# Loads of V issued by SyncE's queue in place of ScalarE's, in an attention and expert kernel

## The chip, the cores and the metric

The kernel runs on one core of a Trainium2 chip. The metric is the device time of one execution in microseconds, the median over several runs. The core's engines each work through their own instructions in a fixed order and wait for each other by semaphores: TensorE (PE in the profile; PEld are its weight loads), VectorE (DVE), ScalarE (ACT), GpSimd (POOL) and SyncE (SP), which does nothing but issue transfers. ACT and POOL can issue transfers too. All transfers of the core are carried by its 16 DMA engines.

## What is computed

Attention over 4 batches of 8 heads with 768 positions and 64 dimensions, in which a query sees only the keys with the same 6-bit hash; then, per batch, the 128 positions with the highest gate score go through one two-layer expert and are added back.

```python
q_bits = (np.einsum('bhsd,dk->bhsk', q, proj) > 0)      # same for k_bits
mask = q_bucket[:, :, :, None] == k_bucket[:, :, None, :]
scores = np.where(mask, scale * np.matmul(q, k.transpose(0, 1, 3, 2)), -1000000000.0)
scores = scores - np.max(scores, axis=-1, keepdims=True)
attn = np.exp(scores)
attn = attn / (np.sum(attn, axis=-1, keepdims=True) + 1e-09)
out = np.matmul(attn, v)                                 # heads side by side: x
top_idx = np.argpartition(-scores[b], capacity)[:capacity]   # scores[b] = x[b] @ w_gate
h = np.maximum(xe @ w1, 0.0)                             # xe = x[b, top_idx]
out[b, top_idx] = x[b, top_idx] + g[:, None] * (h @ w2)
```

## The kernel before

The 32 heads are worked through one after the other, each over all 768 positions, with several heads in flight. A head h has these steps:

- SP loads its queries and keys into X (`load_x`, line 379, 384 KB). ACT rounds them to half precision (XH, line 501), DVE takes the rest (XL, line 506). PE hashes X (line 473), DVE makes signs of it (sg, sd, lines 490 to 497).
- SP moves the pieces into the operands of the matmuls, within the core's memory, all through `move` (line 513): the signs into A and K (`A<-sg`, `K<-sd`), the halves into A (`A<-XH`), the difference of key halves into K (`K<-xd`), and both into B (`B<-A`, `B<-XL`). There are four buffers each of A and K and two of B.
- PE computes an upper bound for each row's score (`max_unit`, line 649), ACT and DVE take its maximum (me, line 657; mj, line 666), PE turns it (line 676), ACT casts it into `mr` (line 681), and SP moves this row of maxima into row 96 of A (`max_row`, the transfer `A<-mr`, 1.5 KB).
- PE computes the scores `st` with A (line 697) and B (line 701), with the maximum taken off in the same matmul; the line 697 matmuls can't start before `A<-mr` has landed. ACT takes the exp into P (lines 715 and 717), DVE or POOL its rounding rest R (lines 732 and 735), and PE multiplies P and R by V into `av` (line 760). ACT scales the result into x (line 784).

V is loaded for two heads at a time (`load_v`, line 382, 16 loads of 384 KB). The tile that a load lands in has one buffer (`bufs=1`), so a load has to wait until DVE has read the pair before from it. ACT splits the load into the upper halves (`split_vh`, line 562), DVE into the lower ones (`split_vl`, line 568), into one of two operand tiles.

In between run the steps of the expert: its weights W are loaded in 8 pieces of 512 KB by ACT's queue (lines 808 and 813), finished halves of x are written out by ACT's queue (line 829), and the scores make a round trip through memory on SP's queue (lines 870 and 873).

What sets the order is a table, `ORDER`, that lists all steps; the steps are issued in this order to all engines, and each engine, and each queue of transfers, keeps it. A transfer is issued by the engine that the line names, at its place among that engine's own instructions. An engine that comes to a transfer whose inputs or buffer aren't ready stands still there, and so does all that is behind it.

Of the kernel before, what the change touches and what calls it, by code (L numbers as in the profile page):

```python
# [41 lines left out]

WARM = (34, 24, 6, 6)
POOL_R = ((1,), (0, 2), ())
ACT_V = True
ACT_W = True
TURNS = True
PJW = 66
# [196 lines left out]
def body(ctx, tc, qk, v, pj, wg, w1, w2, cst, out):  # L245
# [136 lines left out]
    def load_v(pr):  # L382
        t = sb.tile([P, NC, 2, D], F32, tag="V", name=f"V{pr}", bufs=1)
        (nc.scalar if ACT_V else nc.sync).dma_start(t, v[pr])
        st["V", pr] = t
# [918 lines left out]
```

## Time and profile before

| | before |
|---|---|
| median of 3 runs | 417.01 us (414.02 to 419.23) |
| profiled execution | 415.9 us, span 414.1 us |
| PE busy | 392.2 us, 95% |
| DVE busy | 352.4 us, 85% |
| ACT busy | 332.8 us, 80% |
| POOL busy | 181.6 us, 44% |
| SP's queue of transfers (q1) | 35.58 MB, 31.4% of the 16 DMA engines' span |
| ACT's queue of transfers (q10) | 16.45 MB, 12.6% |
| mean granted TensorE clock | 0.996 |

The span runs from the first to the last instruction; the profiled execution's time is 1.8 us longer. PE is close to busy throughout, but matmuls overlap and their ends are modelled, so the places where another engine's wait ends tell more than the share. Of SP the profile shows no busy time, only when it issued what. Where a time of the trace stands with two decimals it is counted from the start of the span.

### The profile page before, as it was taken

The page shows a single profiled execution, that of the slowest core. Times are in us where ns is not written, and L with a number is a line of the kernel's source. Part 1 is how long each engine was busy: PE and PEld are TensorE (multiplying, and loading weights), DVE is VectorE, ACT ScalarE, POOL GpSimd, SP SyncE. Part 2 cuts the span into 40 slices and gives each one's busy share as a digit, 9 for nine tenths or more (in the row PEclk, how much of TensorE's full clock was granted, in tenths as well). Part 3 has the DMA queues.
Part 4 walks back from the last instruction along what each step waited for, and adds up shares of the span by engine and source line. Part 5 has one row for each costly group of instructions (what it writes and reads, how often), then busy time and mean ns, then how long its engine had stood idle before and what let it go on. Part 6 is the DMA issues. An engine that isn't in the chain of part 4 may idle for free. (4 is left out here: it accounts for less than half of the span.)

```text
span 414.1 us, 14588 instructions
## 1 busy us (share of the span) xinstructions
PE 392.2 (95%) x5734; PEld 276.7 (67%) x5742; DVE 352.4 (85%) x942; ACT 332.8 (80%) x817; POOL 181.6 (44%) x107
## 2 busy tenths in 40 slices
PE   5799999999999799999999999999999899999995
PEld 1555667667676466778566777677666678778782
DVE  5889698879999898898989899999998989749852
ACT  5589999799989789898678898989998887767410
POOL 7624546375735528543352535325525062421020
PEclk9999999999999999999999999999999999999999
DMA  7565466654562656634356446736544325100040
GB/s 231 143 207 136 134 160 183 200 170 145 162 205 81 165 158 170 184 100 121 94 151 207 107 115 170 207 70 176 143 142 134 87 70 165 41 3 2 2 155 26
DMA packets 35736, 55.07 MB, mean 133 GB/s; under 512 B 5972, under 2 KB 26964, under 8 KB 35668
## 3 DMA queue, kind: packets, MB, share of 16 engines
q1 hardware_dynamic: 25252, 35.58, 31.4%
q10 hardware_dynamic: 9680, 16.45, 12.6%
q0 software_dynamic: 736, 2.11, 1.6%
q8 instruction: 45, 0.74, 0.7%
q14 instruction: 23, 0.19, 0.2%
HBM read 25.80 MB, written 7.35 MB: 80 GB/s over the span
## 5 line engine op out<-in xcount | busy, mean ns | idle before, releaser
L735 POOL TENSOR_TENSOR R<-P 128x1536 f16<-128x1536 f32 x46 | 134.6, 2926 | 172.8 <-ACT P L717 39.5
L760 PEld LDWEIGHTS <-P 128*128 128x128 bf16 x2304 | 127.2, 98 | 30.9 <-issue 3.7
L760 PE MATMUL av<-V,P 128*128 128x65 f16 (+2 forms) x2304 | 135.3, 194 | 0.0
L760 PE MATMUL av<-V,R 128*128 128x65 f16 (+1 forms) x1152 | 128.3, 193 | 0.5 <-POOL R L735 0.5
L697 PE MATMUL st<-A 97*128 97x512 f16 (+1 forms) x384 | 119.9, 326 | 4.2 <-DMA A<-mr 2.8
L715 ACT ACTIVATE P<-st 128x512 f32<-128x512 f32 x192 | 111.9, 606 | 13.2 <-PE st L701 6.6
L666 DVE CUSTOM_DVE_ANT_0 mj<-bank,me 128x384 bf16<-128x384 f32 x192 | 102.3, 551 | 22.5 <-PE bank L649 11.5
L701 PE MATMUL st<-B 128*128 128x512 f16 (+1 forms) x384 | 119.6, 326 | 0.0
L657 ACT ACTIVATE me<-bank 128x384 f32<-128x384 f32 x192 | 92.6, 498 | 27.4 <-PE bank L649 16.1
L760 PEld LDWEIGHTS <-R 128*128 128x128 f16 x1152 | 107.4, 99 | 0.9 <-POOL R L735 0.6
L732 DVE TENSOR_TENSOR R<-P 128x768 f16<-128x768 f32 x100 | 97.5, 989 | 2.1 <-ACT P L717 1.6
L649 PE MATMUL bank<-K,A 96*128 96x384 f16 x192 | 60.2, 327 | 3.7 <-DMA B<-A 1.5
L717 ACT ACTIVATE P<-st 128x512 f32<-128x512 f32 x96 | 58.6, 610 | 4.1 <-PE st L701 3.9
L649 PE MATMUL bank<-A 96*128 96x384 f16 x192 | 59.5, 326 | 2.5 <-DVE M L666 1.5
L649 PEld LDWEIGHTS <-A 96*128 96x128 f16 x384 | 34.9, 98 | 25.9 <-issue 8.2
L697 PEld LDWEIGHTS <-A 97*128 97x128 f16 x384 | 37.4, 97 | 21.4 <-issue 5.3
L701 PEld LDWEIGHTS <-B 128*128 128x128 f16 x384 | 37.6, 98 | 16.6 <-issue 2.0
L784 ACT ACTIVATE x<-av,rc 128x64 f32<-128x64 f32 x192 | 44.7, 328 | 0.9 <-DVE rc L772 0.8
L506 DVE SCALAR_TENSOR_TENSOR XL<-X,XH 128x768 f16<-128x768 f32 x31 | 30.3, 976 | 1.9 <-DMA B<-XL 1.9
L501 ACT ACTIVATE XH<-X 128x768 f16<-128x768 f32 x31 | 26.4, 855 | 3.8 <-DMA A<-XH 2.0
L1001 POOL DMA_INDIRECT out_dram<-ye,idx x4 | 4.0, 995 | 34.7 <-DVE ye L1000 34.4
L568 DVE SCALAR_TENSOR_TENSOR V<-V,V 128x768 f16<-128x768 f32 x16 | 17.5, 1093 | 0.1
(136 smaller groups left out, 441.7 us busy)
## 6 DMA issues: line engine op xcount, KB each, us to landing
X<-in_qk_dram SPq DMA_DIRECT2D x31, 384.0 KB
V<-in_v_dram ACTq DMA_DIRECT2D x16, 384.0 KB
B<-A SPq DMA_DIRECT2D x64, 96.0 KB
A<-XH SPq DMA_DIRECT2D x62, 96.0 KB
B<-XL SPq DMA_DIRECT2D x62, 96.0 KB
out_dram<-x ACTq DMA_DIRECT2D x7, 768.0 KB
W<-in_w_dram ACTq DMA_DIRECT2D x8, 512.0 KB
K<-xd SPq DMA_DIRECT2D x31, 48.0 KB
```

The costliest lines, as they stand in the source:

```text
L506: mine(nc.vector.scalar_tensor_tensor(xl, st["X", h], XS, st["XH", h], op0=ALU.mult, op1=ALU.subtract))
L649: nc.tensor.matmul(pt[:, :384], a[0:96, 0, t * P : (t + 1) * P], a[0:96, 1, 384:768] if i else K[h % NA][0:96], start=True, stop=True,)
L657: nc.scalar.activation(me, st["mx", h, t, 0][:, :384], AF.Relu)
L666: nc.vector.tensor_tensor_reduce(out=jk, in0=st["mx", h, t, 1][:, :384], in1=st["me", h, t], op0=ALU.add, op1=ALU.max, scale=1.0 / MS, sca ...
L697: nc.tensor.matmul(pt[:, o : o + n], a[:, 1, c * P : (c + 1) * P], a[:, 0, q0 : q0 + n], start=True, stop=False,)
L701: nc.tensor.matmul(pt[:, o : o + n], bt[:, 1, c * P : (c + 1) * P], bt[:, 0, q0 : q0 + n], start=False, stop=True,)
L715: nc.scalar.activation(pp[:, r, 0:512], pt, AF.Exp, scale=ES)
L717: nc.scalar.activation(pp[:, :, 512:768], pt.rearrange("p (a b) -> p a b", a=2), AF.Exp, scale=ES)
L732: mine(nc.vector.tensor_tensor(t[:, r], pp[:, r], hi_view(pp, r), op=ALU.subtract))
L735: turn(nc.gpsimd.tensor_tensor(t, pp, hi_view(pp, a), op=ALU.subtract))
L760: nc.tensor.matmul(o[:, t, o0:o1], l, vv[:, c, hh, v0 + o0 : v0 + o1], start=False, stop=last and l is lo, skip_group_check=True,)
L784: nc.scalar.activation(x[:, t], o[:, t, 1 : D + 1], AF.Copy, scale=rc[:, t : t + 1])
```

## The change

One switch is turned. `load_v` issues the load from SP in place of ACT, at the same place of the table. Size, destination and all other instructions stay as they are.

```diff
-ACT_V = True
+ACT_V = False
```

In SP's order the 16 loads now stand among the moves. At the load for the second pair of heads, in the first part of the program, SP's order changes as follows (sg and sd are signs, mr is the row of maxima, xd the difference of keys):

```order
 L513 DMA K_98<-sd_184 6x384
 L513 DMA A_97<-sg_183 6x768 x2
+L384 DMA V_460<-in_v_dram 128x768
 L513 DMA A_93<-mr_479 1x6x128
 L513 DMA K_98<-xd_472 64x384
```

The load came in ahead of a row of maxima. At the seventh load, about a third of the way through, SP's order is now this (scores and sbc are the round trip of the expert's scores):

```order
L513 DMA B_100<-XL_2402 64x768 x2
L384 DMA V_2867<-in_v_dram 128x768
L513 DMA K_94<-sd_2693 6x384
L513 DMA A_93<-sg_2692 6x768 x2
L513 DMA K_94<-xd_2830 64x384
L513 DMA A_97<-mr_2889 1x6x128
L873 DMA sbc_2958<-scores 128x768
```

Before, the same rows stood there without the load; it came in ahead of four moves and a row of maxima. At the fifteenth load, three quarters through, SP's order changes like this:

```order
 L513 DMA A_93<-sg_6731 6x768 x2
 L513 DMA A_97<-mr_7120 1x6x128
+L384 DMA V_7200<-in_v_dram 128x768
 L513 DMA B_99<-A_91 64x768 x2
 L513 DMA B_99<-XL_6990 64x768 x2
```

Here the load came in behind the row of maxima. ACT's order loses its 16 rows; at the same place it reads (P is the exp, me a maximum, x the scaled result):

```order
 L717 ACTIVATE P_0_7062<-st_2_7115 128x2x256
 L657 ACTIVATE me_5_7181<-bank_65 128x384
-L384 DMA V_7200<-in_v_dram 128x768
 L657 ACTIVATE me_3_7202<-bank_66 128x384
 L784 ACTIVATE x_6931<-av_6964,rc_7183 128x64 x3
```

The activations around it keep their order, as do all instructions of PE, DVE and POOL.

## Rows read from the trace of the kernel before

**Rows 1.** The page, busy time, share of span and instructions of each engine.

```profile
PE 392.2 (95%) x5734; PEld 276.7 (67%) x5742; DVE 352.4 (85%) x942; ACT 332.8 (80%) x817; POOL 181.6 (44%) x107
```

**Rows 2.** Waits: engine, line, what ended them, us in total, times, longest.

```profile
PE st L697 <- DMA A<-mr: 2.8, 5, 0.9
```

**Rows 3.** Issues of lines 384 and 379: ns shortest/median/longest, first and last start.

```profile
L384 ACTq DMA_DIRECT2D V<-in_v_dram x16: 334/336/362, 4.5 to 328.8; - x16
...
L379 SPq DMA_DIRECT2D X<-in_qk_dram x31: 333/530/1253, 1.9 to 288.7; - x31
```

**Rows 4.** Timeline near 320: start us, us, engine (q: its queue), line, operation, [idle before].

```profile
318.55 0.68 SPq L513 DMA_DIRECT2D A<-mr  x1
318.56 0.58 ACT L717 ACTIVATE P<-st 128x512 f32<-128x512 f32 x1
...
318.77 0.34 ACTq L384 DMA_DIRECT2D V<-in_v_dram  x1
...
319.05 0.46 ACT L657 ACTIVATE me<-bank 128x384 f32<-128x384 f32 x1
...
322.15 0.38 PE L697 MATMUL st<-A 97*128 97x512 f16 x1 [1.22 <-ACT x L784]
```

**Rows 5.** Busy us per engine in a stretch; last: clock, DMA share, GB/s.

```profile
319.50:321.50 2.00, 1.43 (x11) 0.68 (x7) 1.83 (x8) 1.76 (x8) 1.06 (x1) 1.00 0.62 197
```

**Rows 6.** Timeline near 226, a row of maxima, a load of V, PE.

```profile
224.14 0.74 SPq L513 DMA_DIRECT2D A<-mr  x1
...
224.44 0.33 ACTq L384 DMA_DIRECT2D V<-in_v_dram  x1
...
227.79 0.38 PE L697 MATMUL st<-A 97*128 97x512 f16 x1 [0.53 <-DMA A<-mr]
```

**Rows 7.** Timeline near 310, a row of maxima without a load of V beside it.

```profile
309.00 0.67 SPq L513 DMA_DIRECT2D A<-mr  x1
...
310.75 0.39 PE L697 MATMUL st<-A 97*128 97x512 f16 x1 [0.57 <-DMA A<-mr]
```

**Rows 8.** Timeline from 133.5 to 139.6: SP's issues, the cast of mr, PE.

```profile
133.59 1.14 SPq L513 DMA_DIRECT2D B<-XL  x2
...
134.77 0.75 SPq L513 DMA_DIRECT2D K<-sd  x1
...
135.48 0.24 ACT L681 CAST mr<-bank 6x128 f16<-6x128 f32 x1
...
135.56 1.42 SPq L513 DMA_DIRECT2D A<-sg  x2
...
137.09 0.52 SPq L513 DMA_DIRECT2D K<-xd  x1
...
137.70 0.69 SPq L513 DMA_DIRECT2D A<-mr  x1
...
139.45 0.39 PE L697 MATMUL st<-A 97*128 97x512 f16 x1 [0.56 <-DMA A<-mr]
```

**Rows 9.** Timeline from 29 to 34.1: SP's issues, ACT's split of V, PE.

```profile
29.00 1.48 SPq L513 DMA_DIRECT2D A<-sg  x2
...
31.05 0.68 SPq L513 DMA_DIRECT2D A<-mr  x1
...
33.53 0.84 ACT L562 ACTIVATE V<-V 128x768 f16<-128x768 f32 x1
...
34.05 0.38 PE L697 MATMUL st<-A 97*128 97x512 f16 x1
```

**Rows 10.** Timeline from 152 to 163.5: SP's issues, DVE's read of V, PE.

```profile
152.21 0.42 SPq L379 DMA_DIRECT2D X<-in_qk_dram  x1
...
153.04 0.94 DVE L568 SCALAR_TENSOR_TENSOR V<-V,V 128x768 f16<-128x768 f32 x1
...
157.97 1.33 SPq L513 DMA_DIRECT2D B<-XL  x2
...
163.45 0.38 PE L701 MATMUL st<-B 128*128 128x512 f16 x1
```

## The prediction

> **What bounds the kernel now.** I read the page's busy shares first. TensorE (PE) is busy for 95% of the span, VectorE (DVE) for 85%, ScalarE (ACT) for 80% [rows 1]. All of PE's work stands in one fixed order, so nearly every microsecond in which PE stands still is a microsecond of the span, and a DMA matters only where PE, or an engine that PE is about to wait for, stands waiting for it. The second view is the list of waits. The only DMA that PE waits for repeatedly is `A<-mr`, the row of maxima that has to lie in A before the score matmuls of a head (line 697) may start: 5 waits, 2.8 us together [rows 2]. None of the listed waits is for a load of V. So V's own arrival is not late today, and the change can act only through three things: what ScalarE stops doing, what SyncE (SP) has to do in addition, and which transfers lie beside or ahead of which.
>
> The third view is the timeline, at the places where a load of V is issued close to an `A<-mr`. At 318.55 us SP issues `A<-mr`, at 318.77 ACT issues a load of V, and PE starts the score matmul that needs the row only at 322.15, after 1.22 us of idleness [rows 4]. The view puts this wait down to ACT's `x` at line 784, but a score matmul reads nothing of `x`, and the last exp that could hold its bank is the one at 318.56. I read it as a wait for the row, which was then 3.60 us under way. In the two microseconds from 319.5 to 321.5 the DMA engines moved 197 GB/s, 394 KB, just the size of one load of V (384 KB is 393 thousand bytes) [rows 5]. The same picture stands at 224.14 (row), 224.44 (V) and 227.79 (PE, after 0.53 us idle): 3.65 us [rows 6]. Without a load beside it the same transfer takes 1.75 us from issue to the matmul that waits for it, at 309.00 to 310.75 [rows 7] and at 137.70 to 139.45 [rows 8]. A load of 384 KB in flight beside it thus costs a row of maxima about 1.85 us, although the two come from two different queues.
>
> **What is removed: 16 issues on ACT.** Each is 336 ns of ACT's sequencer [rows 3], 5.4 us together. I price them at nothing. At 318.77 the issue lasts until 319.11, while the activation before it works until 319.14 and the next has begun at 319.05 [rows 4]: the engine never stands still. The cover is ACT's own queue of work. If that cover were gone the 5.4 us would be the bound of the gain.
>
> **What is added: 16 issues on SP.** A load of the same size on SP, that of X, takes 0.33 to 1.25 us to issue, median 0.53 [rows 3]. I take 0.53: everything behind it in SP's order moves back by half a microsecond until SP next stands idle. The order of all other engines is unchanged, as is the number of bytes, so the sum has a line for each place where this meets a wait.
>
> - *V behind the row of maxima (318.8 and 224.4).* In SP's order the load now stands right behind `A<-mr`, so it is issued about 0.7 us after it. If the row then goes through as it does alone, it is there at 318.55 + 1.75 = 320.30 and at 225.89. PE was free for it at 322.15 - 1.22 = 320.93 and at 227.79 - 0.53 = 227.26, so both waits fall away whole: -1.22 - 0.53 = **-1.75**. Bound on the other side: 0, if the load still overtakes, or if PE then waits for ACT instead.
> - *V in a full stretch of SP's queue (134.8).* From 133.59 SP issues one move after the other. The `A<-mr` of 137.70 was ready when ACT had cast it at 135.48 + 0.24 = 135.72, so it is SP itself that it waits for, and PE waits for it at 139.45 [rows 8]. The load of V now stands ahead of four moves and this row: +0.53, rounded **+0.5**. Bounds: 0.33 (shortest issue) and 1.25 (longest).
> - *V ahead of the row (30.5).* SP comes to this load after `A<-sg`, at 29.00 + 1.48 = 30.48. A load of V takes at most about 3.4 us (318.77 to 322.15 and 224.44 to 227.79, where the row came with it [rows 4, 6]), so it is there at about 33.9. ACT splits it at 33.53 [rows 9]: 0.4 us late. The `A<-mr` behind it is issued at about 31.1, as before, but now has the load ahead of it: at the measured 3.6 us it is there at 34.7, against 34.05 at which PE wants it, 0.65 late; at 1.75 us it isn't late at all. Bounds 0 and 0.65; I take the 0.4 of ACT, **+0.4**.
> - *V that waits for its buffer (152.7).* V's landing tile exists once, and DVE reads the previous pair from it at 153.04 to 153.98, so no queue can issue the load before that. SP reaches it at 152.21 + 0.42 = 152.63 and stands still for 1.35 us, with ten transfers queued behind, the pair of `B<-XL` at 157.97 the last. With the issue they all move back by 1.9 us. The last `B<-XL` starts at about 158.6 and would now start at 160.5; PE uses it at 163.45 [rows 10], 2.9 us later. Alone it would be in time, behind a load (3.6 us) it would be 0.7 late. Bounds 0 and 0.7; it is nearer to in time, since the load is long through by then: **+0.2**.
> - *The other eleven places.* PE's five waits for a row [rows 2] include none that stands behind a load of V there. I price them at nothing; the cover is the distance between a move's arrival and its use. If all of it were gone, the price would be 11 x 0.53 = 5.8.
>
> Sum: -1.75 + 0.5 + 0.4 + 0.2 = -0.65. The profiled execution took 415.9 us (span 414.1 and 1.8 around it), so by its own time the change comes to 415.25. That execution is 1.1 below the median of the runs, 417.0, and they spread from 414.0 to 419.2. Against the median the same difference gives **416.3**.
>
> A rule of the Trainium skill bears on this, and against the change. The page "DMA: Bandwidth & Descriptors", section "Queues, rings and completion order", says that each DMA engine takes turns between the queues for which it has work, a packet at a time, while within one queue it takes descriptors in order. By that rule a row of maxima on SP's queue would slip through beside a load on ACT's queue, and would stand fully behind it once both are on SP's. The trace agrees only in part: beside a load on the other queue the row took 3.60 and 3.65 us and not 1.75. The rule taken whole gives the slower rival below.
>
> **The rivals.**
> *Nothing that can be seen.* The row takes as long with the load behind it as beside it, or ACT, busy through the same stretch, becomes what PE waits for; and the losses hide too. For it speaks that ACT has work without a gap from 318.56 to 319.5 and that its share is 80%. 417.0.
> *Slower: one queue for all.* Whatever stands behind a load of V in SP's queue pays the 1.85 us that today only two rows pay. It decides where the use comes less than that after the present arrival. At seven places the next row of maxima stands at most four moves behind the load; if all seven paid in full, 7 x 1.85 = 13.0, 430. With the gain struck out and the three losses left (0.5 + 0.4 + 0.2 = 1.1) it is 418.1; with a third of the 13.0 on PE, 4.3, it is 421.3. Against it: the row issued at 31.05 is wanted at 34.05 [rows 9], 3.0 us later, so that of the 3.6 us behind a load only 0.6 would count there.
> *ACT gains.* The issues did cost ACT their 5.4 us, and PE's waits for ACT shrink with it: 411.6. Against it stands the activation that begins while the issue still lasts [rows 4].
>
> **How the numbers follow.** The forecast (small gains and small losses, 414.5 to 418) has 0.50. Nothing seen has 0.20, slower through one queue 0.25 (some 0.05 of it beyond 2%), ACT's gain 0.05. The range reaches from the forecast with its full gain and a low run, 417.0 - 1.75 less the 3.0 by which the lowest run lies under the median, 412.3, to a third of the slower rival, about 421.5; outside lie ACT's gain and the rest of the slower rival, under 2 in 10. A measurement of this kernel can tell about 2% (8 us) from no change. Faster by that much 0.02, within it 0.93, slower 0.05.
>
> **What would show it.** In the profile after: no load of V on ACT's queue; at the head that starts near 320 and the one near 226 PE no longer idle ahead of line 697; near 139 PE's wait for `A<-mr` about half a microsecond longer; near 153 SP standing still until DVE has read the old V; ACT's busy time and gaps the same. I would be wrong if PE shows new waits for `A<-mr` behind loads of V at the eleven places, or if ACT's line 562 starts to wait for V.

## The result, and the profile after

The change makes the kernel slower by about 0.6%: 420.17 us in the median of 22 runs (416.18 to 424.51) against 416.85 of 22 runs of the kernel before (413.77 to 421.38), ratio 1.0062 with a 95% interval of 1.0035 to 1.0089, or 2.6 us (the medians of all runs differ by 3.3). Timed a second time it gave 1.0042 (0.9999 to 1.0086). The forecast was 416.3, a little faster; the measured time lies in its range, but the kernel became slower and not faster. Ratios and intervals throughout are those of the comparisons, which leave out runs more than 1.5% above a kernel's fastest, so that a ratio need not be the quotient of the medians, which are of all runs.

| | before | change | change, second time |
|---|---|---|---|
| profiled execution | 415.9 us, span 414.1 | 421.47 us, span 419.7 | 417.5 us, span 415.7 |
| mean granted TensorE clock | 0.996 | 0.986 | 0.989 |
| SP's queue (q1) | 35.58 MB, 31.4% | 41.87 MB, 36.2% | |
| ACT's queue (q10) | 16.45 MB, 12.6% | 10.16 MB, 7.3% | |

The page of the changed kernel has the busy times that answer [rows 1]. ACT's time is the same to 0.3 us, so 16 issues less gave it nothing back; PE's own time grew by 2.7 us at the same number of matmuls.

```profile
PE 394.9 (94%) x5734; PEld 276.8 (66%) x5742; DVE 354.7 (85%) x942; ACT 333.1 (79%) x817; POOL 181.3 (43%) x107
```

The list of PE's waits answers [rows 2]. The waits for the row of maxima are as long as before though two of them should have gone, and new ones stand beside them, for ACT and of line 649.

```profile
PE st L697 <- DMA A<-mr: 3.0, 6, 1.0
PE bank L649 <- issue: 2.5, 1, 2.5
...
PE st L697 <- ACT P L715: 0.7, 1, 0.7
```

The issues of line 384 answer [rows 3]. The median is 485 ns, close to the 0.53 us assumed; the longest is 1107.

```profile
L384 SPq DMA_DIRECT2D V<-in_v_dram x16: 334/485/1107, 3.2 to 334.2; - x16
```

The two places that carried the forecast answer [rows 4] and [rows 6]. Near 326 the row goes out at 325.62, the load of V behind it at 326.41, and PE starts the score matmul at 327.45, 1.83 us after the row's issue (3.60 before):

```profile
325.62 0.69 SPq L513 DMA_DIRECT2D A<-mr  x1
...
326.41 0.38 SPq L384 DMA_DIRECT2D V<-in_v_dram  x1
...
327.45 0.38 PE L697 MATMUL st<-A 97*128 97x512 f16 x1 [0.28 <-DMA A<-mr]
```

Near 232 the matmul starts 2.95 us after the row's issue and waits for nothing:

```profile
230.18 0.75 SPq L513 DMA_DIRECT2D A<-mr  x1
...
231.03 0.37 SPq L384 DMA_DIRECT2D V<-in_v_dram  x1
...
233.13 0.38 PE L697 MATMUL st<-A 97*128 97x512 f16 x1
```

So the gain came: PE's waits at the two places fell from 0.53 to nothing and from 1.22 to 0.28. To see what ate it, the start of each PE instruction was set against the start of the same instruction in the trace of before (PE's order is the same). Where the difference grows, time was lost. The table lists the steps of over 0.2 us from 44 us on.

| place (us before) | forecast | change | second profile | what ends PE's wait |
|---|---|---|---|---|
| 53 to 65 | 0 | -0.98 | -0.78 | shorter waits, in nearly every kernel below: that execution of before was late here |
| 81.7, load #3 | 0 | +0.85 | +0.96 | ACT's exp |
| 139.5, load #6 | +0.5 | -0.1 | +0.71 | row of maxima |
| 144, line 649 | 0 | +1.01 | +0.51 | `A<-XH` |
| 144 to 147, half clock | 0 | +1.4 | +1.4 | none, matmuls last longer |
| 163.2, load #7 | +0.2 | +0.68 | +0.59 | row of maxima |
| 213.8, load #9 | 0 | +0.58 | +0.64 | DVE, itself late for `B<-XL` |
| 227.8, load #10 | -0.53 | -0.69 | -0.69 | (wait gone) |
| 235 to 237, behind #10 | 0 | +1.0 | +0.7 | row of maxima |
| 322.1, load #14 | -1.22 | -0.95 | -1.33 | (0.28 of the wait left; gone) |
| 322 to 333, behind #14 | 0 | +0.28 | +0.66 | ACT, lines 715 and 657 |

The start, up to 44 us, is left out of it. There the two profiles of the change lie 2.6 us behind and 1.9 ahead of the one of before, and so do the kernels below whose start is untouched (by -0.9 to +4.3 us): the stretch in which the granted clock is at 1.2 GHz begins at 17 to 19 us in some executions and at 27 to 32 in others, and is 3.4 to 10.2 us long.

### The profile page after: what moved, and what is told of

Its sections match the earlier page's. It is cut to its first block, busy times and chain, and to the rows that moved or that the text cites. A ratio compares the mean times of both kernels' runs of the same rounds, so it can differ in the third digit from the quotient of the medians.

```text
span 419.7 us, 14599 instructions
## 1 busy us (share of the span) xinstructions
PE 394.9 (94%) x5734; PEld 276.8 (66%) x5742; DVE 354.7 (85%) x942; ACT 333.1 (79%) x817; POOL 181.3 (43%) x107
## 3 DMA queue, kind: packets, MB, share of 16 engines
q1 hardware_dynamic: 27556, 41.87, 36.2%
q10 hardware_dynamic: 7376, 10.16, 7.3%
## 5 line engine op out<-in xcount | busy, mean ns | idle before, releaser
L760 PEld LDWEIGHTS <-P 128*128 128x128 bf16 x2304 | 129.4, 98 | 30.8 <-issue 3.7
L760 PE MATMUL av<-V,P 128*128 128x65 f16 (+2 forms) x2304 | 137.8, 195 | 0.0
L760 PE MATMUL av<-V,R 128*128 128x65 f16 (+1 forms) x1152 | 130.6, 194 | 2.2 <-DVE R L732 1.7
L760 PEld LDWEIGHTS <-R 128*128 128x128 f16 x1152 | 108.6, 99 | 2.8 <-DVE R L732 1.9
L732 DVE TENSOR_TENSOR R<-P 128x768 f16<-128x768 f32 x100 | 100.3, 1017 | 2.8 <-ACT P L717 2.3
```

Of the source, the lines that this page charges most:

```text
L732: mine(nc.vector.tensor_tensor(t[:, r], pp[:, r], hi_view(pp, r), op=ALU.subtract))
L760: nc.tensor.matmul(o[:, t, o0:o1], l, vv[:, c, hh, v0 + o0 : v0 + o1], start=False, stop=last and l is lo, skip_group_check=True,)
```

## The experiments

Five theories stand in the expectations. Theory 1: places in SP's in-order queue, where loads gain or lose. Theory 2: the granted clock, which falls behind longer waits of PE. Theory 3: scatter of the two executions. Theory 4: the completion semaphores of the transfers. Theory 5: loads #2, #4, #5 and the wait near 144 us. Each kernel was timed beside the kernel before, whose medians were 417.14 us (beside the four groups), 416.59 (load #3 alone, the small load, the two landing tiles, load #14), 416.15 (the change without load #3, loads #2, #4 and #5, the three causes taken away, the second run of (6, 7)) and 418.18 (the change once more, the broadcasts).

Most kernels differ from the one before only in which loads SP issues. The edit, of which below only the numbers stand (counted from 0):

```diff
-ACT_V = True
+SP_V = (10, 14)
-        (nc.scalar if ACT_V else nc.sync).dma_start(t, v[pr])
+        (nc.sync if pr in SP_V else nc.scalar).dma_start(t, v[pr])
```

### The 16 loads in four groups

`SP_V = (10, 14)`, the two behind a row of maxima.

> Only the two loads of V that stand right behind a row of maxima (#10 near 224 us and #14 near 319 us, counted from 0) are issued by SyncE; the other fourteen stay on ScalarE. Theory 1 (order in SyncE's queue: these two places gain, others lose more): about 1.8 us faster, ratio 0.996, and in the profile no idle time of TensorE ahead of line 697 near 227 us, some 0.5 us left near 322 us. Theory 2 (TensorE's granted clock falls because of longer idle stretches, not the queue as such): no longer idle stretch is made here, so the clock stays as before and the time is the same or up to 1.8 us faster. Theory 3 (nothing gained at these two places; what the profile after shows there is scatter): ratio 1.000.

Measured: 417.10 us, ratio 0.9971 (0.9924 to 1.0018). The trace has both gains, -0.69 and -1.18, and gives 0.7 of the first one back at the next head. The weight load of line 697 there, ahead of its matmul:

```profile
238.67 0.10 PEld L697 LDWEIGHTS <-A 97*128 97x128 f16 x1 [0.72 <-DMA A<-mr]
```

Between the two rows of maxima SP issues one move after the other, here with the load of V among them:

```profile
225.80 0.74 SPq L513 DMA_DIRECT2D A<-mr  x1
226.96 0.35 SPq L384 DMA_DIRECT2D V<-in_v_dram  x1
227.37 0.76 SPq L513 DMA_DIRECT2D K<-sd  x1
228.18 1.38 SPq L513 DMA_DIRECT2D A<-sg  x2
229.67 1.15 SPq L513 DMA_DIRECT2D B<-A  x2
230.92 1.84 SPq L513 DMA_DIRECT2D B<-XL  x2
```

From row to row SP took 10.35 us (225.80 to 236.15) where it took 9.71 before (224.14 to 233.85): 0.4 for the load and 0.3 for the pair of `B<-XL`, which took 1.56 before. PE came out of the first row earlier, SP did not, so PE met SP's queue one head later. The point estimate is on Theory 1's side of 1, but the interval holds both theories.

`SP_V = (6, 7)`, run twice, since the profiled execution of the first took 782.76 us and shows nothing of the places.

> Only loads #6 and #7 (near 135 and 153 us) on SyncE. Theory 1: loses what the profile of the change shows at these two places, +0.9 ahead of line 649 near 147 us and +0.7 ahead of the row of maxima near 168 us, together +1.6 us, ratio 1.004. Theory 2: the longer idle stretch near 147 us is followed by a stretch at half the clock (1.2 GHz) in the profile, which adds 1.4 us: +3.0 us, ratio 1.007; without that stretch +1.6. If both places hide it: 1.000.

> Loads #6 and #7 on SyncE once more, for the places in the trace. Theory 1: line 697 near 139 us waits 0.5 us longer for its row than in the kernel before (0.56 there), line 697 near 168 us waits about 0.5 us where it did not; together 1.0 to 1.3 us, ratio 1.003. Theory 2: a wait of over 2.5 us near 144 us and the clock at half behind it come with load #6: 2 us more.

Measured: 418.34 us, 1.0038 (0.9999 to 1.0078), and 418.58, 1.0110 (1.0043 to 1.0176) from 4 runs. The second trace shows only part of it: no longer wait near 139, line 649 near 144 with 1.71 us (1.53 before) and no fall of the clock, and 0.28 near 163. The runs lean to a loss (the first interval just holds 1, the second is from few runs), and in this one trace Theory 1's places hold less than it said.

`SP_V = (0, 1)`, the start.

> Only loads #0 and #1 (at the start and near 30 us) on SyncE. Theory 1: the row of maxima and ScalarE's split of V behind load #1 come late, +0.4 us, ratio 1.001. Theory 2: the start runs as in the profile of the change, full clock earlier, then a half-clock stretch near 29 to 36 us that is 3.4 us longer than before: +2.5 us, ratio 1.006. If what the profile shows there was scatter of that one execution: 1.000.

Measured: 417.28 us, 1.0001 (0.9957 to 1.0045). Theory 2 falls here: in this trace the half clock lies at 31.9 us and PE is 2.3 us behind by 44, but so it is in the traces of (10, 14) and of (14), where the start is as before. What the first pair of profiles shows at the start is scatter.

`SP_V = (2, 3, 4, 5, 8, 9, 11, 12, 13, 15)`, priced at nothing.

> The ten loads that I priced at nothing (#2 to #5, #8, #9, #11 to #13, #15) on SyncE, the other six stay on ScalarE. My forecast: 0, ratio 1.000. Theory 1: they cost what the profile of the change shows at them: -0.9 near 54, +0.8 near 82, +0.6 near 214, +1.0 near 243, +0.1 near 265, +0.3 near 333 us, together +1.9 us, ratio 1.0045. Theory 2: 1.000 while the clock stays as before.

Measured: 418.07 us, 1.0020 (0.9982 to 1.0059), which holds both the 1.000 of the forecast and the 1.0045 of Theory 1. The four groups together give -0.3 + 0.4 + 0 + 0.2 = +0.3%, which fits the change's 0.6 and 0.4 within the intervals. In the trace PE lost 1.11 us at 81.7 and 2.3 near 144, the latter though load #6 is on ACT here.

### Load #3: a store that waits for another transfer's semaphore

In the changed kernel ACT stands still for 1.98 us near 82, where it did not before:

```profile
80.24 0.60 ACT L715 ACTIVATE P<-st 128x512 f32<-128x512 f32 x1
82.30 0.41 ACTq L829 DMA_DIRECT2D out_dram<-x  x1
82.81 0.84 ACT L501 ACTIVATE XH<-X 128x768 f16<-128x768 f32 x1 [1.98 <-DMA A<-sg]
```

No load of V is in ACT's order any more; what is late is the store of x. The list of ACT's instructions with what each waits for, before and after:

```
before:  L829 DMA out_dram<-x_725 128x6x256 [waits DMAHW0_49]
change:  L829 DMA out_dram<-x_725 128x6x256 [waits DMAHW1_49]
```

The program gives its transfers eight completion semaphores in rotation, in the order in which it has written them, and an issue waits until the transfer that had its semaphore last is through. In the kernel before, load #3 is numbered behind the store, in the change three moves ahead of it (eleven of the sixteen loads move up like this by one to six places, and load #1 moves down). The store so gets the next semaphore, that of the second half of `B<-XL`, which lands 3 us after the first. ACT's exps stand behind the store, and PE waits for them.

`SP_V = (3,)`:

> Only load #3 (near 80 us) on SyncE. In the kernel before, ScalarE's store of x at line 829 (issued at 78.63) waits for the first half of B<-XL (there at 77.7); the completion semaphores go round among eight in the written order of the DMAs, and with the load of V placed ahead of the store, the store waits for the second half of B<-XL instead (there at 80.7 in the kernel before, 82.3 in the change). Theory 4 (completion semaphores): ScalarE stands still for about 2 us ahead of line 501 near 81 us, TensorE's line 697 loses 0.8 to 1.0 us there, ratio 1.002. Theory 1 (only places in SyncE's queue): no wait on ScalarE there, 1.000. If the store's issue is late as Theory 4 says but nothing waits behind it: 1.000 with the store at about 82.

Measured: 416.25 us, 1.0030 (0.9990 to 1.0069). The wait is there: ACT's line 501 stood 2.09 us, ended by `B<-XL`, and PE lost 0.95 at line 697.

All loads on ACT as before, and one small load of SP's own, which shifts the rotation by one:

```diff
     def put_out(b, half):
+        if (b, half) == (0, 0):
+            tiny = cp.tile([1, 16], F32, name="tiny")
+            nc.sync.dma_start(tiny, cst[0:1, 0:16])
```

> All loads of V stay on ScalarE as before. One extra load of 64 bytes, which nobody reads, is issued by SyncE just ahead of the store of x of batch 0 (near 77 us), so that the store gets the next completion semaphore, that of the second half of B<-XL. Theory 4: the store is issued 2 us or more later than after the work ahead of it, ScalarE stands still for about 2 us ahead of line 501 near 81 us and TensorE loses 0.8 to 1.0 us ahead of line 697, with no load of V moved. Rival (a load of V on SyncE's queue is what makes it late): the store is issued as before, no wait there; at most the 0.3 to 0.5 us that the extra issue takes on SyncE.

Measured: 417.78 us, 1.0049 (0.9998 to 1.0099). ACT stands still for 1.69 us at the same place (lines are 3 higher in this kernel), and PE loses 0.83:

```profile
77.06 0.60 ACT L715 ACTIVATE P<-st 128x512 f32<-128x512 f32 x1
78.83 0.41 ACTq L832 DMA_DIRECT2D out_dram<-x  x1
79.35 0.85 ACT L501 ACTIVATE XH<-X 128x768 f16<-128x768 f32 x1 [1.69 <-DMA K<-sd]
```

So it is the rotation that does it at this place, not a load of V in SP's queue. The reverse test is the change with load #3 alone put back on ACT:

> The change with load #3 alone put back on ScalarE. Theory 4 (completion semaphores in the written order): the store of x near 82 us waits for the first half of B<-XL again, ScalarE's wait of 2 us ahead of line 501 and TensorE's 0.8 ahead of line 697 go, ratio 1.004 where the change has 1.006. If other loads on SyncE make the store late all the same: the wait stays, 1.006.

The store goes out at once and the wait is gone, as Theory 4 says:

```profile
75.79 0.60 ACT L715 ACTIVATE P<-st 128x512 f32<-128x512 f32 x1
75.80 0.41 ACTq L829 DMA_DIRECT2D out_dram<-x  x1
76.31 0.84 ACT L501 ACTIVATE XH<-X 128x768 f16<-128x768 f32 x1
```

Its time does not follow: 419.39 us, 1.0112 (1.0057 to 1.0167) from 6 runs. The trace lost 0.8 near 144 with the half clock behind it, and 1.57 at load #7, where the change lost 0.68. Whether a PE that is earlier by one mended place meets SP's queue harder at the next is not shown by it.

### Load #7: SP's queue stands behind a buffer

In the changed kernel SP stands still from 157.41 to 158.79 until DVE has read the old V, and the row of maxima goes out at 166.91, where the last pair of moves ahead of it took 2.32 us (1.33 before [rows 10]):

```profile
156.99 0.42 SPq L379 DMA_DIRECT2D X<-in_qk_dram  x1
158.79 0.33 SPq L384 DMA_DIRECT2D V<-in_v_dram  x1
...
164.49 2.32 SPq L513 DMA_DIRECT2D B<-XL  x2
166.91 0.74 SPq L513 DMA_DIRECT2D A<-mr  x1
```

PE has to wait for it:

```profile
168.69 0.38 PE L697 MATMUL st<-A 97*128 97x512 f16 x1 [0.52 <-DMA A<-mr]
```

The change with two landing tiles for V:

```diff
-        t = sb.tile([P, NC, 2, D], F32, tag="V", name=f"V{pr}", bufs=1)
+        t = sb.tile([P, NC, 2, D], F32, tag="V", name=f"V{pr}", bufs=2)
```

> All loads of V on SyncE as in the change, but with two landing tiles for V in place of one, so that load #7 need not wait for VectorE's read of the previous pair and SyncE doesn't stand still there for 1.3 us. Theory 1 (the stall of SyncE's queue makes the row of maxima near 168 us late): the wait ahead of line 697 there (0.52) goes, 0.7 us less than the change: ratio to the kernel before 1.0045. If the row is late because of the bytes of V ahead of it in the same queue: the wait stays, ratio 1.006.

Measured: 417.76 us, 1.0059 (1.0019 to 1.0100). The place behaves as Theory 1 says: SP doesn't stand, the pair of `B<-XL` takes 1.38 us again, and PE waits for nothing at the row that goes out at 162.01:

```profile
153.22 0.42 SPq L379 DMA_DIRECT2D X<-in_qk_dram  x1
153.69 0.42 SPq L384 DMA_DIRECT2D V<-in_v_dram  x1
...
159.48 1.38 SPq L513 DMA_DIRECT2D B<-XL  x2
162.01 0.74 SPq L513 DMA_DIRECT2D A<-mr  x1
```

The runs can't tell 0.7 us from none.

What the 2.32 us were is seen in the trace's packets. One packet of 16 KB on the instruction queue (45 in all, one for about 255 of PE's 11,476 matmuls and weight loads) was carried from 165.06 to 166.44, and SP's issue of the second half of the pair, begun at 165.14, ended at 166.81, 0.37 later. Of the 15 issues of such a 96 KB move that took over 0.85 us in this trace (0.59 is the median of all), 11 ended 0.37 to 0.40 us after such a packet's end; the others are pairs near 170 and 224. That the packet holds the issue up is inferred from these ends. The second profile of the change and the change without load #3 have it at this pair too (1.57 and 1.56 us for the second half), the kernel before and the one with two tiles, where the pair is out before the packet comes, do not. So the load's wait costs SP 1.4 us, and being late costs it 1 us more.

### Load #14 alone

> Only load #14 (near 320 us, behind a row of maxima) on SyncE. Theory 1: the wait of 1.2 us ahead of line 697 near 322 us falls by 0.8 to 1.1 and little is given back, 0.8 us faster, ratio 0.998; unlike load #10, whose gain was taken back by the next row of maxima, since SyncE's queue has no gap between the two. If nothing is gained: 1.000.

Measured: 416.45 us, 1.0019 (0.9973 to 1.0065). In the trace PE gains 1.38 near 322 (the row of maxima leaves at 319.62, the matmul starts at 321.50 without a wait) and loses 0.7 of it by 333, behind ACT's lines 715 and 657. A net of 0.7 is left there; the runs neither show nor exclude it.

Is it the queue that frees the row, or the moment at which the load goes out? In the change both differ: load #14 and load #10 stand on the row's own queue, and they are issued 0.79 and 0.85 us behind the row where they were issued 0.22 and 0.30 behind it. Two traces part the two. In the kernel with the small load, load #10 goes out on ACT's queue 0.53 us behind the row, and in the kernel before with the broadcasts on ACT (the end of this section) load #14 goes out on ACT's queue 0.73 behind it. PE waits for neither row:

```profile
223.25 0.74 SPq L513 DMA_DIRECT2D A<-mr  x1
223.78 0.34 ACTq L384 DMA_DIRECT2D V<-in_v_dram  x1
226.43 0.38 PE L697 MATMUL st<-A 97*128 97x512 f16 x1
```

```profile
322.09 0.68 SPq L513 DMA_DIRECT2D A<-mr  x1
322.82 0.34 ACTq L384 DMA_DIRECT2D V<-in_v_dram  x1
324.82 0.38 PE L697 MATMUL st<-A 97*128 97x512 f16 x1
```

By their semaphore events these rows had landed 1.75 and 1.69 us after their issue, against 3.61 and 3.46 at the same two places of the kernel before. Over all traces, loads #10 and #14 left the row 2.9 to 3.8 us under way where they were issued from 0.51 us ahead of it to 0.33 behind it (16 cases, all on ACT's queue), and 1.69 to 1.75 where they were issued 0.53 to 1.16 behind it (18 cases, these two on ACT's queue). So it is the later moment that frees the row; that the load has to stand on SP's queue for it is not shown.

### Line 649 near 144, and the clock

In the kernel before, PE waits 1.53 us there. The list of waits puts this down to `B<-A`, but line 649 reads A, and the last part of the `A<-XH` ahead of it lands 0.09 us before PE starts: at 143.91, in the change at 147.26, in its second profile at 143.42, while `B<-A` lands after PE has started. The granted clock is full in the stretches around it (columns: us, busy us and instructions of PE, PEld, DVE, ACT, POOL, then PEclk, DMA share, GB/s):

```profile
140.00:144.00 4.00, 2.48 (x29) 1.49 (x27) 3.46 (x14) 1.72 (x5) 2.19 (x1) 1.00 0.69 194
144.00:148.00 4.00, 4.00 (x81) 3.36 (x82) 2.93 (x9) 3.61 (x8) 0.00 (x0) 1.00 0.73 204
148.00:152.00 4.00, 3.92 (x60) 2.81 (x59) 3.90 (x17) 3.28 (x10) 2.00 (x1) 1.00 0.49 135
```

In the change PE waits 2.54 us (to 147.35), is busy for only 1.46 of the four microseconds, and the next four have a mean clock of 0.57, most of them at 1.2 in place of 2.4 GHz:

```profile
144.00:148.00 4.00, 1.46 (x24) 1.12 (x23) 2.15 (x9) 1.30 (x2) 0.65 (x1) 1.00 0.42 105
148.00:152.00 4.00, 4.00 (x65) 3.58 (x65) 2.73 (x7) 2.90 (x7) 0.00 (x0) 0.57 0.73 211
```

The matmuls of that stretch start 1.4 us later by its end. Here too a packet of the instruction queue is carried while the move that PE waits for is under way. In the stretch from 142.5 to 147.7 it is 2.2% of the 16 engines' time, 1.8 us of one engine (in the kernel before 1.3% of 16 x 4.5, 0.9 us):

```profile
q8 instruction: 1, 0.02, 2.2%
```

The pair of `A<-XH` that SP issues beside it takes 2.79 us (1.72 before):

```profile
143.21 1.19 SPq L513 DMA_DIRECT2D B<-A  x2
144.44 2.79 SPq L513 DMA_DIRECT2D A<-XH  x2
```

In the semaphore events of both traces 15 of the 16 parts of the `A<-XH` ahead of that `B<-A` are there early; the last comes 1.0 to 1.1 us after the packet has ended, and the last ones of `B<-A` up to 0.6 later. That it is the same DMA engine I infer from this agreement, not from a row. Of the first nine traces the change, the ten loads and the two landing tiles had the long wait and the fall, so loads #2, #4, #5, common to them, were tried alone (the change without #3 showed the same wait and fall then):

> Only loads #2, #4 and #5 on SyncE. In the three kernels that have these there, the wait of line 649 near 144 us was 2.5 to 2.6 us, with the granted clock at 1.2 GHz for 3.4 us behind it; in six without them 1.5 to 1.9 and the clock stayed. Theory 5 (these loads cause it): 2.5 us and the fall again, ratio 1.004. If it is scatter (one DMA engine that is busy with a 16 KB packet of the instruction queue when A<-XH and B<-A come): 1.5 to 1.9 us, ratio 1.000.

Measured: 419.02 us, 1.0115 (1.0043 to 1.0187) from 4 runs; in the trace 1.41 us of wait and the full clock behind it:

```profile
142.00:146.00 4.00, 2.92 (x30) 1.72 (x29) 3.51 (x13) 2.08 (x4) 2.56 (x1) 1.00 0.67 207
146.00:150.00 4.00, 3.67 (x77) 3.22 (x78) 2.86 (x9) 3.55 (x7) 0.00 (x0) 1.00 0.80 207
```

Theory 5 falls as far as these loads by themselves go; why the runs are slower than this trace is open. The three kernels with 4 to 6 runs (this one, the second run of (6, 7), the change without load #3) all come out at 1.011, whatever they move, and were set against the same runs of the kernel before; by the medians they are 0.6 to 0.8% above it. An offset that the three share is not excluded, so no ratio of theirs by itself shows what its loads cost. Next the change with the named causes taken away (loads #3 and #6 on ACT, two landing tiles):

> The change with three causes taken away: load #3 and load #6 on ScalarE as before, and two landing tiles for V so that load #7 needn't wait for VectorE. If these are the most of it (0.85 near 82 us, 0.5 near 139 us, 0.7 near 168 us, 2.05 together): 2.6 - 2.05 = 0.5 us slower than before, ratio 1.001. If the longer wait for B<-A near 144 us and the stretch at half the clock behind it (2.0 us in the change, seen with loads #2, #4, #5 on SyncE too) are a cause of their own, they stay and the ratio is 1.004 to 1.005.

Measured: 417.08 us, 1.0053 (1.0018 to 1.0088). The steps at 82, 139 and 168 are gone, the wait near 144 is 1.81 with the full clock; behind 44 us this trace is 1.0 us ahead of that of before, between the kernels with (6, 7) and (10, 14) moved (0.6 and 1.3 ahead). The ratio doesn't confirm it: it is near that of the change, with a median 0.9 us over that of the kernel before in the same comparison. Then the change itself once more:

> The change itself, profiled and timed once more. If the longer wait near 144 us belongs to the change: 2.5 us ahead of line 649 and the granted clock at 1.2 GHz behind it again, ratio 1.006. If it belongs to the single execution: 1.6 to 1.9 us there, no fall of the clock, and a profiled time some 2 us under the first one's against its start; the ratio stays at 1.006 if most runs have it, the rest of the loss being near 82, 168 and 243 us either way.

Measured: 418.70 us, 1.0042 (0.9999 to 1.0086). The wait was 2.04 us, between the two cases, and the fall came again; the steps near 82, 163, 214 and 237 are there as well (table above). So these belong to the change, and the length of the wait near 144 differs from one execution to the next.

Last, the three broadcasts of the scores, which stand ahead of `A<-XH` and `B<-A` in SP's queue there, on ACT's queue: in the change, in the kernel before, and in the kernel with load #14 on SP.

```diff
-        nc.sync.dma_start(
+        nc.scalar.dma_start(
             sbc.rearrange("p t k -> p (t k)"), scr[b : b + 1].broadcast_to([P, NC * P])
```

> The change, with the three broadcasts of the scores (line 873) issued by ScalarE in place of SyncE. If the broadcast ahead of A<-XH and B<-A in SyncE's queue makes the wait near 144 us: it falls from 2.6 us to 1 or less, the clock stays at 2.4 GHz behind it, 2 us or more faster than the change, ratio to the kernel before 1.000 to 1.001. If the wait comes from the packet of the instruction queue alone: it stays at 1.6 to 2.6, ratio 1.006. If ScalarE has to wait for the scores at line 873, exps come late and it is slower than the change.

> The kernel before (all loads of V on ScalarE) with the three broadcasts of the scores on ScalarE. By the same reasoning the wait of 1.6 us near 144 us falls to 1 or less and SyncE's queue is 0.4 us shorter at three places: 0.6 to 1.6 us faster, ratio 0.996 to 0.9985; by the rivals 1.000, or slower if ScalarE waits at line 873.

> The kernel before with load #14 on SyncE, behind the row of maxima, and the broadcasts of the scores on ScalarE: the one gain that held in the traces and the one that the wait near 144 us promises, 0.8 + 0.6 to 1.6 = 1.4 to 2.4 us faster, ratio 0.994 to 0.997. If the gain at #14 is given back behind it as the runs of that kernel alone leave open (1.0019 with an interval of 0.9973 to 1.0065): as the kernel with the broadcasts alone.

Measured: 419.46 us, 1.0052 (1.0010 to 1.0094); 417.55, 1.0021 (0.9978 to 1.0064); 416.31, 0.9978 (0.9935 to 1.0020). The wait near 144 does fall, in the kernel before from 1.53 to 0.36, and it comes back behind it: ACT's load of W (line 813) is held at its issue, which the list of instructions again shows with a semaphore that it didn't wait for before (DMAHW1), and PE waits for ACT. ACT and PE of that kernel, the broadcasts on ACT:

```profile
149.22 0.39 ACTq L813 DMA_DIRECT2D W<-in_w_dram  x1
149.66 0.49 ACT L657 ACTIVATE me<-bank 128x384 f32<-128x384 f32 x1 [1.98 <-DMA B<-A]
```

```profile
146.35 0.32 PE L649 MATMUL bank<-K,A 96*128 96x384 f16 x1 [0.36 <-issue]
150.20 0.32 PE L649 MATMUL bank<-A 96*128 96x384 f16 x1 [1.32 <-ACT me L657]
```

In the change the wait moved ahead instead, to line 697 at 142.03 with 2.34 us: the broadcast, itself 384 KB, goes out on ACT at 138.72, 0.17 us ahead of the row of maxima, and the row lands 3.10 us after its issue. The granted clock fell behind this wait, at 143.01, though the expectation had it stay. The kernel with load #14 shows the same two things (2.48 us of wait, 6.8 us at 1.2 GHz from 143.13), the kernel with the broadcasts alone, where the broadcast goes out 0.42 behind the row, neither. The gain expected of the first did not come. The interval of the second reaches only the small end of what was expected (0.9985), that of the third holds all of it, and no gain as well. No version was found that beats the kernel before beyond its interval; the last one is the lowest beside loads #10 and #14 alone.

## Why the prediction was wrong

- *What was removed.* Right: ACT's busy time and gaps gained nothing from 16 issues less. The place in ACT's order mattered in another way (load #3).
- *V behind the row of maxima, -1.75.* Right where it was said: -1.64 and -2.02 in the two profiles of the change, the row through 1.83 us after its issue near 326, close to the 1.75 that it takes alone. The reason given, two queues beside each other, is only half of it: with the load on ACT's queue the row is as fast once the load goes out 0.5 us later. Wrong in that the gain stays. Behind #10 all of it came back within 10 us, since SP issues without a gap up to the next row; behind #14 0.3 to 0.7 came back through ACT. Of the 1.75 some 0.4 to 0.7 is left.
- *V in a full stretch (#6), +0.5.* 0.71 in one profile of the change, 0.52 with two landing tiles, 0.50 without load #3, nothing in the first: right in mechanism and about in size.
- *V ahead of the row (#1), +0.4.* Not seen: SP issued the load at 27.79, not 30.5, and the row at 31.72 was the next, 3.93 us behind it. Loads #0 and #1 alone give 1.0001, and ACT's line 562 never waits for V in either profile.
- *V that waits for its buffer (#7), +0.2.* The mechanism was right, the size not: 0.6 to 0.7, and it was not the last `B<-XL` but the row of maxima behind it that PE waited for. I had priced the 1.35 us of standing, not what the moves behind it then fall on: the last of them took 1 us longer to issue beside a packet of the instruction queue.
- *The other eleven places at nothing.* This is the step that failed: the order of the other engines stayed, but not what they wait for. At #3 a store got another completion semaphore and ACT waited (PE: 0.85 and 0.96). At #9 the load stands ahead of `A<-XH`, X and `B<-XL` in SP's queue, and DVE waits for the last (PE: 0.58 and 0.64):

```profile
218.56 0.96 DVE L506 SCALAR_TENSOR_TENSOR XL<-X,XH 128x768 f16<-128x768 f32 x1 [0.80 <-DMA B<-XL]
```

  The cover that I named, the distance between arrival and use, was never read place by place. The runs of the ten loads alone (1.0020) neither show nor exclude these losses; the traces show them at their places.
- *The clock* stood in no term. A wait of PE that grew near 144 was followed by 3.4 us at 1.2 GHz in both profiles of the change, 1.4 us more. How often that happens in the runs is not known.
- *The rivals.* "One queue for all" gave 418.1 to 421.3 and is the one that came true in size and in one or two of its three named losses (#7 in both profiles, #6 in one, #1 in none), not in its mechanism: the gain was there too, and a row right behind a load did not pay 1.85 (the row of 273.14, 0.63 behind load #12 on the same queue, landed after 2.66, 0.9 more than alone). What paid was whatever came last in a gapless stretch of SP's queue.

The steps of the first pair of profiles sum to +4.0 behind 44 us without the step near 53 to 65, those of the second to +4.3; the runs say 2.6 and 1.75. One execution each is not enough for a sum: the wait near 144 alone went from 1.4 to 1.9 us among the kernels with at most three loads moved. That the losses at 82, 168 and 214 to 243 are of the change is shown by both profiles, for 82 also by the kernels that make and unmake it, and for 168 by the one that unmakes it; that near 144 is only shown to come often with it. The 0.6% itself is not traced to these places by the runs: the kernel with three of them mended came out at 1.0053.

## What to carry to other kernels

Before a transfer is moved to another queue, read at every one of its places what the receiving queue does until its next idle moment: in a stretch without a gap any gain at its head is met again at its end. Ask, too, whether issuing the transfer half a microsecond later on its old queue would do the same; here it did in two traces. Look at the list of waits of the changed program too, since moving one transfer renumbers the completion semaphores of the ones around it, and an in-order engine that also issues transfers then stands still for a transfer it has nothing to do with. And profile the same kernel twice, or kernels with an untouched stretch, before a step of one trace is put down to the change.

## What the runs showed of the hardware that was not expected

- Where the stretch at 1.2 GHz falls in the first 38 us is different from execution to execution of kernels with the same start, and PE is 1.9 us ahead to 4.3 behind at 44 us by it, more than the change is worth.
- A row of maxima beside load #10 or #14 (384 KB) lands 1.69 to 1.75 us after its issue where the load is issued 0.53 to 1.16 us behind it, on either queue, and after 2.9 to 3.8 where it is issued from 0.51 ahead to 0.33 behind, on the other queue. The Trainium skill's page "DMA: Bandwidth & Descriptors", section "Queues, rings and completion order", has the turn-taking between queues and the order within one that the prediction named. By the turn-taking alone the row should slip past in both cases; here it did so only with half a microsecond's start, and the order within one queue delayed what stood behind the load.
- A 16 KB packet of the instruction queue, carried by one DMA engine in 0.9 to 1.8 us, goes with a long issue of SP's move beside it, which ends 0.37 to 0.40 us after the packet (11 of 15 long issues in the change). It comes at about the same instruction of PE each time, so shifting SP's queue by 1 us decides which move it meets.
- The granted clock fell to 1.2 GHz near 144 in the seven traces with a wait of 2.0 to 2.5 us there, with PE little busy around it, and stayed full in the other ten, behind waits of up to 1.8.
